# Chunk bounds of k from rows of half chunks and k's score operand by DMA, for half of the head pairs of a fused attention and feed-forward kernel

## The chip, the cores and the metric

The kernel runs on one core of one Trainium2 chip. The metric is the time on the device in microseconds (us), the median of several runs. A run can also be profiled: the profile then shows one execution, with every instruction of the five engines (PE, the matrix engine; DVE, the vector engine; ACT, the scalar engine; POOL, the general engine; SP, which here only issues transfers) and every transfer.

## The reference

The program is a chunk-selecting attention, whose output feeds a gated feed-forward layer. Batch B = 4, heads H = 8, sequence S = 768, head width D = 64, feed-forward width 1536.

```python
k_min, k_max = k_chunks.min(axis=3), k_chunks.max(axis=3)     # chunks of 32 rows of k
ub = sum_d(max(q * k_min, q * k_max))                         # per query and chunk, then a causal mask
top_chunks = argsort(ub)[..., -6:]                            # the 6 best chunks of each query
scores = (q @ k.T) / 8, kept where the chunk is chosen and the position is causal
attn = softmax(scores) @ v
x = attn with the heads side by side: 3072 tokens of 512
xn = x / sqrt(mean(x*x) + 1e-6) * rms_g
out = (silu(xn @ w_gate) * (xn @ w_val)) @ w_out
```

## The kernel before

The work is cut into 16 pairs of heads (four pairs a batch) and 8 halves of a batch for the feed-forward layer (`f0.0`, `f0.1`, ... `f3.1`). Every step (`Step`) names the engine or engines that may do it, a guess of its duration, what it depends on and the buffers that it opens and uses. A planner (`Order.run`) walks through a modelled time and, whenever an engine is free, gives it the ready step of the lowest rank; a rank is a place from `TIMES` plus an offset per kind from `RANK`. The result is one fixed instruction order per engine, which the chip then follows in order. `SLOTS` says how many buffers of each kind there are, and a step cannot be planned while its buffer is taken.

`prep` readies a pair, here for both k and q:

- `kload`, `qload`: two transfers on SP's queue bring the two heads' rows, 128 positions on the partitions, into a `nat` buffer (line 479).
- `kT`, `qT`: six fp32 transposes on PE (line 498) into PSUM, and `kE`, `qE`: two evictions by ACT or DVE (lines 294 and 298), so that d lies on the partitions: 64 rows for each of the two heads, 768 columns (`kt`, `qt`).
- `kmx`, `kmn`: two reductions on DVE over the chunks of `kt` (lines 524 and 526), then `dif`.
- `kC`, `qC`: four casts on POOL (line 298) into the bf16 operands of the scores, `KE` and `QS`. The 64 other rows of `KE` hold a constant 0 / -30000 pattern `e_all`, those of `QS` the selection.
- `relu`, `ub`, `ubE`, `up`, `ubm`, `max`, `sel`, `selT`, `selC`: the bounds, the six best chunks of each query, and the selection turned into `QS`.

`scores` then does the score matmuls (`sc`, line 718), the exponential on ACT (`exp`, line 735), and attention times v (`av`, line 754); `norm_out` divides (`xb`). `norm` scales the rows of half a batch (`sq`, `eps`, `root`, `xs`) and turns them, for batch 0 by PE (`tp`, line 848), for the others by DMA transposes on SP's queue (`xT`, line 837). `ffn` does the feed-forward matmuls (`gate` line 882, `val` line 903, `po` line 923), with `tanh` on ACT and `tg`, `hh` on DVE.

PE also has 48 steps `busy` (line 341): matmuls of zeros of 512 columns with a rank of 1000 and more, which the planner puts wherever nothing else is ready for PE; all of them fall in the first 29 us. The first feed-forward matmul waits for the first half of batch 0, that is for the scores of the first four pairs, so the kernel has a first stage without the large matmuls.

Of the kernel before, what the change touches and what calls it, by code (L numbers as in the profile page):

```python
# [8 lines left out]
FP32 = mybir.dt.float32  # L9
BF16 = mybir.dt.bfloat16  # L10
ALU = mybir.AluOpType
ACT = mybir.ActivationFunctionType
AXX = mybir.AxisListType.X
# [11 lines left out]

RANK = (
    dict(
        av=156.13, dif=-333.01, eps=-30.9, exp=-297.75, kC=249.04, kE=-171.16, kT=-97.43,
        kload=1.5, kmn=-85.09, kmx=75.56, max=-238.74, qC=324.63, qE=-109.16, qT=-140.07,
        qload=45.82, relu=246.29, root=261.37, sc=129.21, sel=17.88, selC=51.2, selT=55.02,  # L30
        sq=-363.37, tp=-68.78, tpE=108.05, ub=-155.85, ubE=-484.91, ubm=-159.09, up=-350.79,
        vload=-102.18, xb=-100.78, xs=-3.48,
    ),
    dict(
        av=8.1, dif=164.62, eps=-549.11, exp=227.88, gate=-37.01, hh=-145.73, kC=-36.47,
        kE=243.85, kT=-61.3, kload=39.2, kmn=324.05, kmx=284.92, mask=143.91, max=194.96,
        out=-122.32, po=137.5, poE=216.04, qC=234.68, qE=-450.99, qT=88.22, qload=32.32,
        relu=163.99, root=-883.1, sc=-22.64, sel=-113.94, selC=20.01, selT=-328.58, sq=384.43,
        tanh=51.44, tg=-50.58, ub=10.99, ubE=298.61, ubm=-119.37, up=-28.2, val=-0.94,
        vload=151.14, xT=-62.62, xb=39.12, xs=-64.22,  # L40
    ),
)

TIMES = {
# [15 lines left out]
}  # L60


# [139 lines left out]
def kernel(  # L202
# [11 lines left out]
    nc = tc.nc  # L214
    P = nc.NUM_PARTITIONS
    B, H, S, D = q.shape
    assert (P, D) == (128, 64) and S == 768
    CH = 32
    NCH = S // CH
    NT = S // P  # L220
# [6 lines left out]
    KM = D + NCH + 1  # L227
    W = S // 2
    G = 3
    NPAIRS = B * NP  # L230

    SLOTS = dict(ps=8, nat=8, vext=4, set=3, ku=3, selq=3, qt=7, ubs=2, small=8, ubm=3,
                 pt=10, xb=2, xt=2, row=3, xs=4, ff=8, hh=36, ob=3)

    def limits(sub, t):
        return LIMITS[sub][0 if t < FIRST else 1]
# [4 lines left out]
    WHOLE, HALVES = [(0, NT)], [(0, HB), (HB, HB)]  # L241
    PARTS = [WHOLE] * 3 + [HALVES] + [WHOLE] * (NPAIRS - NP)
    FIRST = 42.0
    BUSY = 48
    LIMITS = dict(score=(5, 3), av=(2, 2), prep=(4, 3), ffn=(3, 4), norm=(3, 2), po=(2, 2))
    order = Order(SLOTS, limits)
    order.LIM = LIMITS
# [3 lines left out]
    def add(name, engs, occ, rank, *a, **kw):  # L251
        return order.add(name, engs, occ, rank if isinstance(rank, dict) else {"": rank}, *a, **kw)

    def rank(place, b, kind, n=0, pace=None):
        r = {place: 1.0, f"{kind}.{min(b, 1)}": 1.0}
        if n:
            r[pace] = float(n)
        return r
# [14 lines left out]
    def tile_of(b, shape, dtype, name):  # L273
        pool = ps if b.kind == "ps" else sb
        b.tile = pool.tile(shape, dtype, name=name, tag=f"{b.kind}{b.slot}")
        return b.tile
# [11 lines left out]
    def pe(n):  # L288
        return 0.003 + n / 2400.0
# [20 lines left out]


    KU = [const.tile([P, 2, CH], FP32, name=f"ku{i}") for i in range(SLOTS["ku"])]
    SELQ = [const.tile([P, NT, 2, D], BF16, name=f"selq{i}") for i in range(SLOTS["selq"])]
    VX = [const.tile([P, 2 * NT, D + 1], BF16, name=f"vx{i}") for i in range(SLOTS["vext"])]
    e_all = const.tile([D, S], BF16, name="e_all")
# [19 lines left out]
    zeros = const.tile([P, 4 * P], BF16, name="zeros")  # L335
    c_zero = add("zeros", "DVE", 0.2, -101, lambda e: nc.vector.memset(zeros[:], 0.0))

    def busy(bank):
        def go(e):
            t = tile_of(bank, [P, 4 * P], FP32, "busy")  # L340
            nc.tensor.matmul(t[:], zeros[:, 0:P], zeros[:], start=True, stop=True)  # L341
        return go

    for i in range(BUSY):
        bank = Buf("ps")
        add("busy", "PE", pe(4 * P), 1000.0 + i, busy(bank), [c_zero], opens=[bank])
    c_ku = [add("ku0", "DVE", 0.1, -95 + i, lambda e, i=i: nc.vector.memset(KU[i][:], 0.0))
            for i in range(SLOTS["ku"])]
    c_sel = [add("selq0", "DVE", 0.38, -90 + i, lambda e, i=i: nc.vector.memset(SELQ[i][:], 0.0))
# [27 lines left out]
    c_e = prev  # L377
    c_ke = [None] * NB
    for i in range(NB):
        if i == 0:  # L380
            c_ke[i] = add("ke0", "", {"DVE": 1.05, "ACT": 1.4}, {"ke0": 1.0}, lambda e: (
                evict(e, KE[0][0][D:2 * D, :], e_all[:]),
                evict(e, KE[0][1][0:D, :], e_all[:])), [c_e])
        else:
            c_ke[i] = add("ke", "SP", 1.0, {"ke": 1.0}, lambda e, i=i: (
                nc.sync.dma_start(out=KE[i][0][D:2 * D, :], in_=e_all[:]),
                nc.sync.dma_start(out=KE[i][1][0:D, :], in_=e_all[:])), [c_e], load=180000)

    def make_cmf(n):
        if n == 0:  # L390
# [71 lines left out]
    def prep(c, i0, nb, at, lr):  # L462
# [4 lines left out]
        c0, c1 = i0 * 4, (i0 + nb) * 4  # L467
        nat, big = {}, {}
        done = {}
        for w, src in (("k", k), ("q", q)):  # L470
            nat[w], big[w] = Buf("nat"), Buf("qt")

            def load(e, w=w, src=src, r0=0, rn=nb):
# [44 lines left out]
        def red(e, which, x0, xn):  # L518
            view = big["k"].tile[:, x0 * P:(x0 + xn) * P].rearrange("p (c t) -> p c t", t=CH)
            a0, a1 = x0 * 4, (x0 + xn) * 4  # L520
            if which == 0:
                if mx.tile is None:
                    tile_of(mx, [P, NCH], FP32, "kmx")
                nc.vector.tensor_reduce(out=mx.tile[:, a0:a1], in_=view, axis=AXX, op=ALU.max)
            else:
                nc.vector.tensor_reduce(out=KU[c.ku.slot][:, 0, c0 + a0:c0 + a1], in_=view,
                                        axis=AXX, op=ALU.min)

        reds = []
        step = 3 if p == 0 else nb  # L530
        for x0 in range(0, nb, step):
            after = done["k"][x0 // 3:(x0 + step) // 3]
            lead = {"": -10.0} if p == 0 and x0 == 0 else {}
            reds += [
                add("kmx", "DVE", 0.06 + step * P * 0.00106, {**rank(at, b, "kmx"), **lead},
                    lambda e, x0=x0: red(e, 0, x0, step), after, opens=[mx], uses=[big["k"]]),
                add("kmn", "DVE", 0.06 + step * P * 0.00106, {**rank(at, b, "kmn"), **lead},
                    lambda e, x0=x0: red(e, 1, x0, step), after + c_ku, opens=[c.ku],
                    uses=[big["k"]])]

        def diff(e):
            engine[e].tensor_tensor(
# [5 lines left out]
        c.dif[i0] = df  # L548


        casts = []
        for w, dst in (("k", KE), ("q", QS)):
            for hl in range(2):
                rows = slice(hl * D, (hl + 1) * D)

                def cast(e, w=w, dst=dst, hl=hl, rows=rows):
                    evict(e, dst[c.set.slot][hl][rows, cols], big[w].tile[rows, 0:n])

                casts.append(add(w + "C", "", {e: {"POOL": pool(n), "ACT": act(n)}[e] for e in CASTS[p]},
                                 rank(at, b, w + "C", hl, "step"), cast, done[w], opens=[c.set],  # L560
                                 uses=[big[w]]))
# [131 lines left out]
    def scores(c, i0, nb, at, pace, adds):  # L693
# [3 lines left out]
        for hl in range(2):  # L697
# [5 lines left out]
            for g, (nd, regions) in enumerate(groups):  # L703
# [9 lines left out]
                def score(e, regions=regions, sc=sc, hl=hl, kk=kk, tri=tri):  # L713
# [9 lines left out]
                    if tri:  # L723
# [3 lines left out]
                            start=False, stop=True)  # L727

                need = list(c.sel) + [y for z in c.ke.values() for y in z] + [c_tri] + c_ke
                s = add("sc", "PE", sum(pe(x[2] * P) for x in regions) + (pe(tri * P) if tri else 0),  # L730
                        rank(at, b, "sc", m, pace), score, need, opens=[sc], uses=[c.set])

                def soft(e, sc=sc, pt=pt, nn=nn):
# [14 lines left out]
                def prod(e, pt=pt, todo=todo, av=av, left=left, hl=hl):  # L748
# [4 lines left out]
                    for m, (x, kb, qi) in enumerate(todo):  # L753
# [4 lines left out]

                avs.append(add("av", "PE", 0.029 * nn, rank(at, b, "av", m, pace), prod, [x, c.vload], opens=[av],
                               uses=[pt, c.v]))  # L760

            def norm_out(e, hl=hl, av=av):
                if XB[b].tile is None:
# [222 lines left out]
```

## Time and profile before

| what | value |
|---|---|
| median of 3 runs | 325.68 us (325.23 to 325.82) |
| time of the profiled execution | 326.77 us |
| its span, first to last instruction | 325.1 us |
| mean granted clock of PE | 0.989 |
| PE busy | 316.8 us (97%) |
| DVE busy | 245.1 us (75%) |
| ACT busy | 201.5 us (62%) |
| POOL busy | 118.8 us (37%) |
| HBM read, written | 28.57 MB, 6.29 MB |

[...] The time of the profiled execution lies 1.67 us above its span and 1.09 us above the median.

### The profile page before, as it was taken

What the parts mean: (1) busy time and instruction counts of PE and PEld (TensorE: products, weight loads), DVE (VectorE), ACT (ScalarE), POOL (GpSimd) and SP (SyncE); (2) the same over time, 40 slices, a digit from 0 to 9 for tenths busy, and PEclk for the clock granted to TensorE, in tenths of its full rate; (3) what the DMA queues carried; (4) which work ended last, traced back from release to release, by engine and by line L of the source; (5) the groups of instructions that cost most, each with busy time, mean ns of one, the idle gap of its engine ahead of it and who ended that gap; (6) DMA issues with size and microseconds to landing.
All of it is one profiled execution on the core that took longest, in us unless ns stands there. A gap on an engine that the chain in (4) does not pass through costs nothing.

```text
span 325.1 us, 7875 instructions
## 1 busy us (share of the span) xinstructions
PE 316.8 (97%) x2972; PEld 200.5 (62%) x2972; DVE 245.1 (75%) x664; ACT 201.5 (62%) x434; POOL 118.8 (37%) x170
## 2 busy tenths in 40 slices
PE   8999998999999999999999999999999999999995
PEld 3567865667667767765667667556665466555542
DVE  6789988799789889879998767969767778444500
ACT  5578988575777498993469779755465252333121
POOL 8649426364425764583213556520012000000000
PEclk9999997899999999999999999999999999999999
DMA  9999999798908669857010330150000720011023
GB/s 172 213 216 198 180 198 219 118 191 143 92 0 184 87 106 169 149 140 50 1 50 2 24 28 2 40 123 35 0 2 33 131 65 1 34 65 66 1 79 114
DMA packets 92501, 30.25 MB, mean 93 GB/s; under 512 B 85424, under 2 KB 89264, under 8 KB 92464
## 3 DMA queue, kind: packets, MB, share of 16 engines
q1 hardware_dynamic: 62352, 21.50, 29.8%
q0 software_dynamic: 28512, 7.87, 24.0%
q10 hardware_dynamic: 1600, 0.39, 0.6%
q8 instruction: 23, 0.38, 0.5%
q14 instruction: 14, 0.11, 0.1%
HBM read 28.57 MB, written 6.29 MB: 107 GB/s over the span
## 4 chain that ended last, share of the span: by engine, by line
PE 92%; DVE 4%; DMA 1%; ACT 1%; issue 0%; ACTq 0%
PE gp L882 20%; PE vp L903 19%; PE po L923 19%; PE sc L718 11%; PE av L754 6%; PE ub L586 5%; PE pq L498 3%; PE pk L498 3%; PE busy L341 3%; PE up L610 2%; PE st L655 2%; DMA qnat<-in_q_dram 1%; DVE selq L644 1%; PE tp L848 0%; DVE selq L639 0%
## 5 line engine op out<-in xcount | busy, mean ns | idle before, releaser
L735 ACT ACTIVATE pt<-sc 128x512 bf16<-128x512 f32 (+3 forms) x192 | 90.9, 570 | 7.4 <-PE sc L718 5.2
L889 ACT ACTIVATE sg<-gp 128x384 bf16<-128x384 f32 x96 | 46.9, 493 | 53.1 <-PE gp L882 52.3
L882 PE MATMUL gp<-xT,wg 128*128 128x384 bf16 x384 | 76.1, 331 | 0.0
L903 PE MATMUL vp<-xT,wv 128*128 128x384 bf16 x384 | 75.7, 326 | 0.0
L895 DVE SCALAR_TENSOR_TENSOR tg<-sg,gp 128x384 bf16<-128x384 bf16 x96 | 51.7, 550 | 25.7 <-ACT sg L889 24.8
L923 PE MATMUL po<-wo,hh 128*128 128x512 bf16 x288 | 69.2, 379 | 0.0
L911 DVE TENSOR_TENSOR hh<-vp,tg 128x384 bf16<-128x384 f32 x96 | 52.3, 553 | 9.7 <-PE vp L903 8.6
L718 PE MATMUL sc<-qs,ke 89*128 89x128 bf16 (+5 forms) x420 | 56.7, 256 | 0.5 <-ACT qs L294 0.4
L882 PEld LDWEIGHTS <-wg 128*128 128x128 bf16 x384 | 36.9, 99 | 25.2 <-issue 2.4
L903 PEld LDWEIGHTS <-wv 128*128 128x128 bf16 x384 | 36.0, 98 | 23.1 <-issue 0.8
L741 POOL TENSOR_SCALAR_AFFINE_SELECT pt<-pt 128x512 bf16<-128x512 bf16 (+1 forms) x48 | 26.1, 556 | 63.3 <-ACT pt L735 62.8
L923 PEld LDWEIGHTS <-hh 128*128 128x128 bf16 x288 | 27.3, 98 | 26.7
L754 PE MATMUL av<-vx,pt 128*128 128x65 bf16 x672 | 38.9, 193 | 1.3 <-ACT pt L735 1.3
L754 PEld LDWEIGHTS <-pt 128*128 128x128 bf16 x672 | 32.4, 98 | 10.6 <-ACT pt L735 2.2
L718 PEld LDWEIGHTS <-ke 89*128 89x128 bf16 (+1 forms) x420 | 30.9, 99 | 10.2 <-issue 2.1
L298 POOL CAST qs<-qt 64x768 bf16<-64x768 f32 x30 | 28.3, 944 | 24.3 <-DVE qt L298 13.3
L298 POOL CAST ke<-kt 64x768 bf16<-64x768 f32 x31 | 26.5, 855 | 8.3 <-ACT kt L294 5.9
L296 ACT ACTIVATE osb<-po 128x512 f32<-128x512 f32 x19 | 11.3, 597 | 29.2 <-PE po L923 29.2
L294 ACT ACTIVATE qs<-st 64x768 bf16<-64x768 bf16 x20 | 16.1, 804 | 7.5 <-PE st L655 7.2
L826 DVE SCALAR_TENSOR_TENSOR xs<-xb,ri,gains 128x512 bf16<-128x512 bf16 x24 | 18.3, 797 | 1.5 <-DMA xT<-xs 1.0
L770 DVE TENSOR_TENSOR xb<-av,rden 128x384 bf16<-128x384 f32 (+1 forms) x34 | 18.2, 534 | 1.2
L631 DVE MAX8 m<-ubm 128x8 f32<-128x24 f32 x192 | 18.9, 169 | 0.1
(72 smaller groups left out, 335.8 us busy)
## 6 DMA issues: line engine op xcount, KB each, us to landing
out_dram<-osb SPq DMA_DIRECT2D x24, 256.0 KB, 2.2
knat<-in_k_dram SPq DMA_DIRECT2D x30, 192.0 KB, 4.8
qnat<-in_q_dram SPq DMA_DIRECT2D x30, 192.0 KB, 4.9
vx<-in_v_dram POOLq DMA_DIRECT2D x16, 192.0 KB, 5.2
wo<-in_moe_w_out_dram POOLq DMA_DIRECT2D x2, 768.0 KB, 9.3
wg<-in_moe_w_gate_dram POOLq DMA_DIRECT2D x2, 768.0 KB, 8.8
wv<-in_moe_w_val_dram POOLq DMA_DIRECT2D x2, 768.0 KB, 9.3
ke<-e_all SPq DMA_DIRECT2D x4, 96.0 KB, 3.4
```

The source lines that it names most:

```text
L298: engine[e].tensor_copy(out_, in_)
L498: nc.tensor.transpose(t[:, j * P:(j + 1) * P], nat[w].tile[:, j0 + j].rearrange("p h d -> p (h d)"), ident_f[:])
L718: nc.tensor.matmul(t[:, x:x + m, :].rearrange("p a b -> p (a b)"), ke[kk, kb * P:(kb + 1) * P], qs[kk, q0 * P:(q0 + m) * P], start=not tri ...
L735: nc.scalar.activation(out=t[:, 0:nn, :], in_=sc.tile[:, 0:nn, :], func=ACT.Exp, scale=SCALE)
L741: nc.gpsimd.affine_select(out=pt.tile[:, 0:nd, :], in_=pt.tile[:, 0:nd, :], compare_op=ALU.is_ge, fill=0.0, base=0, pattern=[[0, nd], [1, ...
L754: nc.tensor.matmul(av.tile[:, qi - i0, :], pt.tile[:, x, :], VX[c.v.slot][:, hl * NT + kb, :], start=(begin and m == 0), stop=(left[0] == ...
L882: nc.tensor.matmul(t[:], wg[:, g, hs], XT[b].tile[:, g, cols], start=(g == 0), stop=(g == NP - 1))
L889: nc.scalar.activation(out=t[:], in_=gp.tile[:], func=ACT.Tanh, scale=0.5)
L895: nc.vector.scalar_tensor_tensor(out=t[:], in0=sg.tile[:], scalar=1.0, in1=gp.tile[:], op0=ALU.add, op1=ALU.mult)
L903: nc.tensor.matmul(t[:], wv[:, g, hs], XT[b].tile[:, g, cols], start=(g == 0), stop=(g == NP - 1))
L911: nc.vector.tensor_tensor(out=t[:], in0=vp.tile[:], in1=tg.tile[:], op=ALU.mult)
L923: nc.tensor.matmul(po.tile[:], hhs[ht].tile[:, th * P:(th + 1) * P], wo[:, ht, :], start=(ht == 0), stop=(ht == NHT - 1))
```

## The change

For the last 8 of the 16 pairs (`p >= ROWS`, with `ROWS = 8`) the steps `kload`, `kT`, `kE`, `kmx`, `kmn` and `kC` are replaced:

- `khload` brings the two heads' k as 96 partitions of 16 whole rows each (half a chunk per partition), 1024 numbers of fp32.
- `kmx`, `kmn` reduce each partition over its 16 rows; the reduction reads every 64th number. Their 96 x 128 result is turned by one fp32 transpose on PE, and `join`, four small reductions on DVE, makes the chunks' bounds of the half chunks' and puts them where `dif` and `ub` expect them.
- `kbload` brings k a second time, by two casting transfers on POOL's queue, into the bf16 buffer `KB`, whose other columns hold the pattern `e_all` turned (`eT`, `eC`, done once).
- `kX`: two DMA transposes on SP's queue write `KE` from `KB`, all 128 rows.

After the second head's scores of the third pair come 40 more `busy` matmuls of 256 columns, again of a rank of 1000 and more. All numbers in `RANK` and `TIMES` are new, so the order of everything changes; so are some counts of buffers. The built program has 48 fp32 transposes fewer and 8 others more on PE, 16 casts fewer on POOL, 16 evictions of k fewer on ACT and DVE together.

```diff
-    SLOTS = dict(ps=8, nat=8, vext=4, ..., qt=7, ubs=2, small=8, ubm=3,
-                 pt=10, xb=2, xt=2, row=3, xs=4, ff=8, hh=36, ob=3)
+    ROWS = 8
+    HC = S // (CH // 2)
+    SLOTS = dict(ps=8, nat=6, kh=2, km=2, kb=2, vext=4, ..., qt=6, ubs=2, small=7, ubm=3,
+                 pt=10, xb=2, xt=2, row=2, xs=4, ff=8, hh=30, ob=3)
-    BUSY = 48
+    BUSY, LATER = 48, 40
...
+    KB = [const.tile([P, 2, NT, 2 * D], BF16, name=f"kb{i}") for i in range(SLOTS["kb"])]
+    def turn_e(e):
+            nc.tensor.transpose(t[:, j], e_all[:, j * P:(j + 1) * P], ident_b[0:D, 0:D])
+    def copy_e(e):
+                evict(e, KB[i][:, h, :, (1 - h) * D:(2 - h) * D], et.tile[:])
...
-        for w, src in (("k", k), ("q", q)):
+        rows_k = p >= ROWS
+        for w, src in (("q", q),) if rows_k else (("k", k), ("q", q)):
...
+            def load_h(e):
+                t = tile_of(kh, [2 * HC, CH // 2, D], FP32, "khalf")
+                nc.sync.dma_start(out=t[:], in_=k[b, h0:h0 + 2].rearrange(
+                    "h (c t) d -> (h c) t d", t=CH // 2))
+            def whole(e, which):
+                nc.vector.tensor_reduce(
+                    out=km.tile[:, which], in_=kh.tile[:].rearrange("p t d -> p d t"), axis=AXX,
+                    op=ALU.max if which == 0 else ALU.min)
+            def turn_m(e):
+                nc.tensor.transpose(t[:], km.tile[:].rearrange("p m d -> p (m d)"),
+                                    ident_f[0:2 * HC, 0:2 * HC])
+            def join(e):
+                for m in range(2):
+                    for h in range(2):
+                        nc.vector.tensor_reduce(
+                            out=dst, in_=kt.tile[m * D:(m + 1) * D, h * HC:(h + 1) * HC].rearrange(
+                                "p (c t) -> p c t", t=2),
+                            axis=AXX, op=ALU.max if m == 0 else ALU.min)
+            def load_b(e):
+                for h in range(2):
+                    nc.gpsimd.dma_start(
+                        out=KB[kb.slot][:, h, :, h * D:(h + 1) * D],
+                        in_=k[b, h0 + h].rearrange("(t p) d -> p t d", p=P))
+                def move(e, hl=hl):
+                    nc.sync.dma_start_transpose(
+                        out=KE[c.set.slot][hl][:].rearrange("d (t p) -> d t p", p=P),
+                        in_=KB[kb.slot][:, hl].rearrange("p t d -> p (t d)"))
...
+            if p == 2 and hl:
+                for i in range(LATER):
+                    bank = Buf("ps")
+                    add("busy", "PE", pe(2 * P), 1000.0 + i, busy(bank, 2 * P), [last_sc], opens=[bank])
```

More of the change, by code (lines that the diff above doesn't have):

```diff
@@ L27 @@
     dict(
[L28 to L32, printed above, removed]
+        av=43.57, dif=-30.29, eps=179.06, exp=-200.01, kC=120.21, kE=-311.62, kT=-305.1,
+        kload=-105.22, kmn=-185.9, kmx=-27.69, max=-21.8, qC=182.72, qE=166.19, qT=-206.09,
+        qload=-84.21, relu=243.91, root=91.35, sc=-70.23, sel=-65.8, selC=94.24, selT=-324.14,
+        sq=169.36, tp=-132.93, tpE=221.19, ub=-176.21, ubE=-58.41, ubm=-542.64, up=-208.33,
+        vload=-353.61, xb=196.99, xs=-231.93,
     ),
     dict(
[L35 to L40, printed above, removed]
+        av=-55.49, dif=107.31, eps=-219.18, exp=76.29, gate=-52.44, hh=-476.39, join=12.45,
+        kC=221.56, kE=-131.64, kT=36.75, kX=16.24, kbload=-12.11, khload=45.16, kload=89.93,
+        kmn=249.43, kmx=151.07, mask=-188.09, max=127.02, out=-169.48, po=80.53, poE=187.61,
+        qC=167.85, qE=-80.09, qT=54.86, qload=78.72, relu=-304.43, root=-329.97, sc=64.55,
+        sel=15.85, selC=-282.78, selT=-64.95, sq=-40.96, tanh=168.5, tg=-70.57, ub=-23.31,
+        ubE=-254.01, ubm=22.75, up=-154.86, val=-25.56, vload=159.79, xT=-132.02, xb=55.59,
+        xs=92.8,
     ),
@@ L229 @@
     G = 3
+    ROWS = 8
+    HC = S // (CH // 2)
     NPAIRS = B * NP
-    SLOTS = dict(ps=8, nat=8, vext=4, set=3, ku=3, selq=3, qt=7, ubs=2, small=8, ubm=3,
-                 pt=10, xb=2, xt=2, row=3, xs=4, ff=8, hh=36, ob=3)
+    SLOTS = dict(ps=8, nat=6, kh=2, km=2, kb=2, vext=4, set=3, ku=3, selq=3, qt=6, ubs=2, small=7, ubm=3,
+                 pt=10, xb=2, xt=2, row=2, xs=4, ff=8, hh=30, ob=3)
     def limits(sub, t):
@@ L336, with busy @@
     c_zero = add("zeros", "DVE", 0.2, -101, lambda e: nc.vector.memset(zeros[:], 0.0))
-    def busy(bank):
+    def busy(bank, n):
         def go(e):
             t = tile_of(bank, [P, 4 * P], FP32, "busy")
-            nc.tensor.matmul(t[:], zeros[:, 0:P], zeros[:], start=True, stop=True)
+            nc.tensor.matmul(t[:, 0:n], zeros[:, 0:P], zeros[:, 0:n], start=True, stop=True)
         return go
@@ L345 @@
         bank = Buf("ps")
-        add("busy", "PE", pe(4 * P), 1000.0 + i, busy(bank), [c_zero], opens=[bank])
+        add("busy", "PE", pe(4 * P), 1000.0 + i, busy(bank, 4 * P), [c_zero], opens=[bank])
     c_ku = [add("ku0", "DVE", 0.1, -95 + i, lambda e, i=i: nc.vector.memset(KU[i][:], 0.0))
@@ L387 @@
                 nc.sync.dma_start(out=KE[i][1][0:D, :], in_=e_all[:])), [c_e], load=180000)
+    et = Buf("ps", "prep")
+    def turn_e(e):
+        t = tile_of(et, [P, NT, D], BF16, "et")
+        for j in range(NT):
+            nc.tensor.transpose(t[:, j], e_all[:, j * P:(j + 1) * P], ident_b[0:D, 0:D])
+    def copy_e(e):
+        for i in range(SLOTS["kb"]):
+            for h in range(2):
+                evict(e, KB[i][:, h, :, (1 - h) * D:(2 - h) * D], et.tile[:])
+    c_et = add("eT", "PE", 0.2, {"eT": 1.0}, turn_e, [c_e, c_idb], opens=[et])
+    c_kb = [add("eC", "", {"DVE": 4 * 0.28, "ACT": 4 * 0.39}, {"eT": 1.0}, copy_e, [c_et], uses=[et])]
     def make_cmf(n):
@@ L527, in red @@
                                         axis=AXX, op=ALU.min)
[L529 to L539, printed above, removed]
+        reds, casts = [], []
@@ L548, in prep @@
         c.dif[i0] = df
-        casts = []
-        for w, dst in (("k", KE), ("q", QS)):
+        for w, dst in (("q", QS),) if rows_k else (("k", KE), ("q", QS)):
             for hl in range(2):
@@ L729, in scores @@
                 need = list(c.sel) + [y for z in c.ke.values() for y in z] + [c_tri] + c_ke
-                s = add("sc", "PE", sum(pe(x[2] * P) for x in regions) + (pe(tri * P) if tri else 0),
+                s = last_sc = add("sc", "PE", sum(pe(x[2] * P) for x in regions) + (pe(tri * P) if tri else 0),
                         rank(at, b, "sc", m, pace), score, need, opens=[sc], uses=[c.set])
```

36 lines of the change are left out of this document (added), and 30 rows, old and new, of the table TIMES.

## The prediction

> **What bounds the kernel now.** I read the busy shares, the 40 slices and the end of the chain first, then busy time by stretches.
>
> ```profile
> PE 316.8 (97%) x2972; PEld 200.5 (62%) x2972; DVE 245.1 (75%) x664; ACT 201.5 (62%) x434; POOL 118.8 (37%) x170
> PEclk9999997899999999999999999999999999999999
> PE 92%; DVE 4%; DMA 1%; ACT 1%; issue 0%; ACTq 0%
> ```
>
> PE is busy all the time and carries 92% of the chain; the granted clock dips in slices 7 and 8. The stretches (us; busy PE, PEld, DVE, ACT, POOL; then granted clock, DMA share, GB/s) say where PE is not full:
>
> ```profile
> 40.00:48.00 8.00, 7.59 (x128) 5.78 (x127) 7.17 (x29) 6.93 (x16) 1.77 (x3) 1.00 1.08 199
> 48.00:52.00 4.00, 2.47 (x32) 1.45 (x29) 3.73 (x11) 2.99 (x9) 2.94 (x3) 1.00 1.16 201
> 52.00:54.00 2.00, 1.63 (x11) 1.10 (x10) 1.47 (x2) 1.98 (x4) 1.01 (x2) 0.56 1.15 206
> 54.00:58.00 4.00, 4.00 (x23) 2.58 (x22) 2.49 (x8) 3.85 (x10) 1.64 (x3) 0.50 1.25 239
> 58.00:60.00 2.00, 2.00 (x11) 1.05 (x10) 1.11 (x2) 1.01 (x4) 0.24 (x1) 0.73 1.15 201
> 60.00:210.00 150.00, 150.00 (x1645) 101.34 (x1644) 131.11 (x370) 110.76 (x247) 75.89 (x104) 1.00 0.54 79
> ```
>
> Before 60 us, DVE and ACT are almost full and PE waits: 1.5 us of 48 to 52. Then the clock falls to one half, until about 59. From 60 us on PE has no gap: there the time is the sum of PE's matmuls. DVE is next, 131.1 of 150 us (87%), with 18.9 us left; that number decides below. The timeline shows what opens the second stage:
>
> ```profile
> 50.84 2.63 DVE L826 SCALAR_TENSOR_TENSOR xs<-xb,ri,gains 128x512 bf16<-128x512 bf16 x3
> 51.64 0.40 PE L848 MATMUL tp<-ident_b,xs 128*128 128x128 bf16 x4
> 54.92 0.63 PE L848 MATMUL tp<-ident_b,xs 128*128 128x128 bf16 x4
> 55.59 0.42 DVE L298 COPY xT<-tp 128x512 bf16<-128x512 bf16 x1
> 56.06 5.20 PE L882 MATMUL gp<-xT,wg 128*128 128x384 bf16 x22
> ```
>
> The three `xs` end at 53.47; the later transposes stand on PE behind scores at half clock, and the first `gate` starts at 56.06. So the time is the start of `gate`, then PE's remaining work, then a tail after the last matmul that the change does not touch (an eviction and a store).
>
> **The change part by part.** The prices on PE:
>
> ```profile
> 74.82 0.82 PE L498 MATMUL pk<-ident_f,knat 128*128 128x128 f32 x6
> 63.37 0.49 PE L498 MATMUL pk<-ident_f,knat 128*128 128x128 f32 x3
> L724 PE MATMUL sc<-trimask,ident_b 128*128 128x512 bf16 x6 | 2.3, 380 | 0.0
> L724 PE MATMUL sc<-trimask,ident_b 128*128 128x256 bf16 x6 | 1.6, 274 | 0.0
> ```
>
> Three more fp32 transposes take 0.33 us: 0.11 each. 256 more bf16 columns take 106 ns: 0.053 us per 128.
>
> *PE after the first gate.* The program's order says what stands behind the first `gate`. Before, the k transposes of pairs 5 to 15, 66 of them; after, those of pairs 6 and 7, 12, and 8 single ones: 54 x 0.11 = 5.9 us less, 8 x 0.11 = 0.9 more. The first eight score groups of pair 4 (29 blocks of 128 columns) stood ahead of the gate and now stand behind: 29 x 0.053 = 1.5 more. So does the `selT` of pair 4, six blocks: 0.3 more. The half clock after 56.06 (to about 59) cost 1.5 us, which goes if the clock stays full. Sum: -5.9 + 0.9 + 1.5 + 0.3 - 1.5 = -4.7 us.
>
> *The 40 zero matmuls.* 40 x 0.106 = 4.2 us of PE. In the order nine lie among the scores of pair 3 and 31 between its last `av` and the first `tp`, that is in the wait for `xs`. PE's other work ahead of the first `tp` changes by +0.2 (`eT`) and -0.3 (`selT`). Before, PE got to the first `tp` at 51.6 (the row above), having waited 1.5 us in that stretch; 51.6 - 1.5 + 4.2 - 0.1 = 54.2, where the first `xs` would be ready at 50.84 + 0.88 = 51.7 and the third at 53.5. So the zeros cover the wait and cost at most 0.7 us past the third `xs`; without the wait they would cost all 4.2.
>
> *The start of gate.* DVE does more ahead of `xs`: four copies for `eC`, priced by the copy to `xT` below at 0.42 each, 1.7 us; the other steps moved over this line (four evictions of q fewer, four of bounds more, two sums of squares more, two `max` and a `sel` fewer) come to about nothing. With all 1.7 the third `xs` ends at 55.2, and `tp` and a copy at full clock, 0.8, put the gate at 56.0. With none of it, and the zeros, 55.0. Before it was 56.06. I take no change.
>
> *DVE behind it.*
>
> ```profile
> L524 DVE TENSOR_REDUCE kmx<-kt 128x24 f32<-128x768 f32 x15 | 14.1, 943 | 0.7 <-ACT kt L294 0.4
> L524 DVE TENSOR_REDUCE kmx<-kt 128x12 f32<-128x384 f32 x2 | 1.1, 543 | 0.0
> L298 DVE COPY kt<-pk 128x384 f32<-128x384 f32 x8 | 4.4, 555 | 4.4 <-PE pk L498 3.9 <-PE av L754 0.3
> L298 DVE COPY xT<-tp 128x512 bf16<-128x512 bf16 x2 | 0.8, 424 | 1.3 <-PE tp L848 1.3
> L644 DVE TENSOR_SCALAR selq<-m x16: 181/190/858, 16.9 to 221.7; 128x12 bf16<-128x12 f32 x16
> L810 DVE TENSOR_SCALAR ms<-ss x8: 157/169/170, 48.7 to 249.6; 128x3 f32<-128x3 f32 x8
> ```
>
> Between 384 and 768 numbers a reduction grows by 400 ns: 1.04 ns a number over 143 ns. Sixteen reductions of 1024 numbers take 16 x 1.21 = 19.4 us in place of 16 x 0.943 = 15.1. But they read every 64th number. No row has a long strided read. The nearest are the last two: 12 numbers at a stride take a median of 190 ns, 3 adjacent ones 169; 21 ns for nine more, 2.3 ns each, and here the write is strided too. So a reduction lies between 1.21 us and 143 + 1024 x 2.09 = 2.28 us, the double slope; nothing excludes a little more, and less than the contiguous price is excluded because the count of numbers sets it. I take the lower end for the forecast, since twelve numbers are a thin row, and keep the upper one as a rival. `join` is four tiny operations of about 0.17 us (the 169 ns row): 8 x 0.7 = 5.6. Five evictions move from DVE to ACT or go, -2.8. Sum +7: 138 of 150 us, 92%; PE stays the bound. ACT loses 15 evictions of k and gains nine others, so it is no bound.
>
> *POOL and SP.*
>
> ```profile
> L298 POOL CAST ke<-kt 64x768 bf16<-64x768 f32 x31 | 26.5, 855 | 8.3 <-ACT kt L294 5.9 <-DVE kt L298 1.2 <-PE sc L718 0.2
> L456 POOL DMA_DIRECT2D vx<-in_v_dram x16 | 16.8, 1050 | 5.3 <-PE up L610 2.6 <-PE av L754 2.2 <-issue 0.4
> L837 SPq DMA_TRANSPOSE xT<-xs x18: 1190/1216/1682, 130.7 to 260.2; - x18
> DMA to landing us min/median/max: 2.4/2.4/4.0
> ```
>
> POOL drops 16 casts (13.7 us) and issues 16 casting loads of half of `vx`'s size, 0.5 to 1.05 us each, 8 to 17 us: no bound at 76 of 150. A DMA transpose of four blocks occupies SP's queue 1.2 us and lands after 2.4; six blocks by proportion 1.8 and 3.6. A pair's two hold SP 3.6 us, and what waits behind them are loads of later pairs and stores of `out`. The tightest places are pairs 10 and 15, whose operand buffers the previous pair gives back about 7 us of PE work ahead of their first score: 1.8 + 3.6 = 5.4 fits. The second load of k adds about 3 MB to a stage whose DMA share is 0.54.
>
> *Sum.* 326.77 - 4.7 = 322.1 us for a profiled execution, span 320.4. The median stood 1.09 below the profiled time: **321.0 us**.
>
> **The rivals.**
>
> *Strided reductions make DVE the bound.* At 2.28 us the sixteen cost 16 x 1.07 = 17.1 us more: 131.1 + 7 + 17.1 = 155 of DVE work for 150 us of PE work. It decides from about 1.8 us a reduction on, where the 18.9 us of room are used up. PE then waits at `selT`, `po` and the feed-forward's banks: 5 us at least, 8 with two waits' worth of DVE idling left; I put 6.5, that is 327.5 us, slower. For it: the 190 ns row, and a strided memset on POOL below. Against it: both are tiny operations.
>
> ```profile
> L351 POOL MEMSET vx<- 128x12 bf16 x4 | 0.6, 144 | 0.0
> L403 POOL MEMSET trimask<- 128x128 bf16 x1 | 0.2, 197 | 0.0
> ```
>
> (12 scattered numbers take nearly as long as 128 adjacent ones.) [...]
>
> *The clock falls all the same.* PE may still idle between the three `tp` while DVE finishes `xs`, about 0.9 us apart. Before, a stretch with 2.47 of 4 us busy was enough to halve the clock, one with 7.59 of 8 was not. If it falls again, the 1.5 us are not won and up to 1.5 are lost ahead of the gate: 323 us. [...]
>
> *The transposes come late.* If six blocks land at the worst row's rate, 4.0 x 1.5 = 6 us, the two tight places and the loads queued behind cost 1 to 2 us: 322.5. That the change does not do what it says is excluded for the order (the zeros stand where they should); for the clock it is the rival above.
>
> **How the numbers follow.** Forecast 0.42, strided rival 0.38, clock 0.10, late transposes 0.05, something else 0.05. A measurement here can tell 0.2%, 0.65 us. Faster by more: 0.39 + 0.09 + 0.03 + 0.03 (a price halfway) = 0.54; the same: 0.08; slower: 0.31 of the strided rival and the unnamed 0.05 and a little = 0.38. The forecast's own range is 319.0 to 323.5 (gate 1 us earlier, zeros or small waits 2.5 us dearer); the strided rival reaches from 323.5 to 331. Together 319.0 to 329.5.
>
> **What would show it.** Right: `pk` x48, the third slice group at full clock with `gate` near 56 us, reductions near 1.2 us, DVE near 92% in 60 to 210, PE without gaps. Wrong: reductions near 2.3 us with PE waiting for DVE between 100 and 200 us; a clock below 0.9 after 50 us; scores of pairs 10 or 15 waiting for a transpose.

## The result, and the profile after

The changed kernel takes 329.91 us (median of 6 runs, 329.51 to 330.78); the kernel before took 325.9 us beside it (6 runs, 325.23 to 326.93). The ratio is 1.0117, 95% interval 1.0102 to 1.0131: slower by 1.2%. The forecast was 321.0 us, faster. The profiled execution took 330.35 us, its span is 328.6 us.

The busy shares, the granted clock, and the chain that ended last, first by engine, then by line:

```profile
PE 315.7 (96%) x2955; PEld 198.7 (60%) x2978; DVE 258.0 (79%) x690; ACT 198.4 (60%) x424; POOL 119.4 (36%) x174
PEclk9999999999999999999999999999999999999999
PE 68%; DVE 26%; issue 3%; ACT 1%; ACTq 0%
PE po L1011 15%; PE vp L991 14%; PE gp L970 13%; PE sc L801 8%; DVE kmm L564 7%; PE busy L345 5%; PE av L837 4%; DVE tg L983 4%; DVE hh L999 3%; PE ub L669 3%; PE pq L518 2%; DVE m L714 2%; DVE rt L651 2%; DVE xb L858 2%; PE pk L518 1%
```

The clock does not fall in this execution, but DVE now carries 26% of the chain where it had 4%, and the largest line of DVE in it is `kmm`, the strided reductions. Next the groups that the change adds (the number behind the bar is the busy sum, then the mean of one in ns):

```profile
L564 DVE TENSOR_REDUCE kmm<-khalf 96x64 f32<-96x1024 f32 x16 | 30.6, 1917 | 0.0
L587 DVE TENSOR_REDUCE ku<-kmt 64x24 f32<-64x48 f32 x16 | 3.4, 210 | 0.3
L587 DVE TENSOR_REDUCE kmx<-kmt 64x24 f32<-64x48 f32 x16 | 3.1, 195 | 0.1
L575 PE MATMUL kmt<-ident_f,kmm 96*128 96x96 f32 x8 | 1.9, 254 | 1.5 <-DVE rden L857 0.8 <-DVE kmm L564 0.7
```

A strided reduction takes 1.92 us where the forecast put 1.21. The stretches (us; busy PE, PEld, DVE, ACT, POOL; clock, DMA share, GB/s):

```profile
48.00:52.00 4.00, 4.00 (x62) 3.16 (x61) 3.62 (x13) 3.12 (x9) 2.34 (x3) 1.00 1.19 254
60.00:210.00 150.00, 144.40 (x1516) 93.08 (x1527) 139.94 (x380) 99.94 (x217) 71.44 (x100) 1.00 0.87 117
```

The zeros fill the wait at 48 to 52 us. Between 60 and 210 us PE, which had no gap before, lacks 5.6 us, and DVE rose from 131.1 to 139.94. Who it waits for, by the waits of PE behind the first `gate` (us in total, times, longest):

```profile
PE up L693 <- DVE ubs L301: 0.9, 2, 0.7
PE kmt L575 <- DVE rden L857: 0.8, 1, 0.8
PE sc L801 <- DVE hh L999: 0.7, 1, 0.7
PE kmt L575 <- DVE kmm L564: 0.7, 1, 0.7
PE sc L801 <- DVE qs L301: 0.6, 1, 0.6
```

Each of these is short, and most name another DVE operation than `kmm`. The same stretch on both engines shows why:

```profile
200.07 1.89 DVE L564 TENSOR_REDUCE kmm<-khalf 96x64 f32<-96x1024 f32 x1
201.89 0.17 DVE L857 RECIPROCAL rden<-av 128x6 f32<-128x6 f32 x1
202.10 0.27 PE L575 MATMUL kmt<-ident_f,kmm 96*128 96x96 f32 x1 [0.79 <-DVE rden L857]
```

The reduction ends at 201.96 and PE's transpose of its result waits for it; the wait is put down to the reciprocal that came just behind. DVE takes its steps in the planned order: the reciprocal behind this reduction (1.89 us from 200.07) starts only at 201.89, so whatever stands behind a long reduction is late with it.

The time can be split at the first `gate`:

```profile
53.23 0.39 PE L936 MATMUL tp<-ident_b,xs 128*128 128x128 bf16 x4
55.67 2.11 PE L970 MATMUL gp<-xT,wg 128*128 128x384 bf16 x12 [0.95 <-ACT xT L297]
```

`gate` starts at 55.67 (before: 56.06). From there to the end of the span it was 325.1 - 56.06 = 269.0 us; now it is 328.6 - 55.67 = 272.9. All of the loss lies behind the gate.

### The profile page after: what moved, and what is told of

It is laid out like the page before. It is cut to its first block, busy times and chain, and to the rows that moved or that the text cites. A ratio compares the mean times of both kernels' runs of the same rounds, so it can differ in the third digit from the quotient of the medians.

```text
span 328.6 us, 7911 instructions
## 1 busy us (share of the span) xinstructions
PE 315.7 (96%) x2955; PEld 198.7 (60%) x2978; DVE 258.0 (79%) x690; ACT 198.4 (60%) x424; POOL 119.4 (36%) x174
## 4 chain that ended last, share of the span: by engine, by line
PE 68%; DVE 26%; issue 3%; ACT 1%; ACTq 0%
PE po L1011 15%; PE vp L991 14%; PE gp L970 13%; PE sc L801 8%; DVE kmm L564 7%; PE busy L345 5%; PE av L837 4%; DVE tg L983 4%; DVE hh L999 3%; PE ub L669 3%; PE pq L518 2%; DVE m L714 2%; DVE rt L651 2%; DVE xb L858 2%; PE pk L518 1%
## 5 line engine op out<-in xcount | busy, mean ns | idle before, releaser
L818 ACT ACTIVATE pt<-sc 128x512 bf16<-128x512 f32 (+3 forms) x192 | 88.2, 572 | 10.1 <-PE sc L801 7.0
L1011 PE MATMUL po<-wo,hh 128*128 128x512 bf16 x267 | 66.3, 379 | 1.3 <-issue 0.3
L801 PE MATMUL sc<-qs,ke 89*128 89x128 bf16 (+5 forms) x418 | 52.4, 250 | 1.5 <-DVE hh L999 0.7
L801 PEld LDWEIGHTS <-ke 128*128 128x128 bf16 (+1 forms) x420 | 29.9, 97 | 12.8 <-issue 3.2
L837 PEld LDWEIGHTS <-pt 128*128 128x128 bf16 x672 | 30.2, 98 | 8.8 <-issue 1.2
L837 PE MATMUL av<-vx,pt 128*128 128x65 bf16 x672 | 34.4, 193 | 0.1
L301 POOL CAST qs<-qt 64x768 bf16<-64x768 f32 x30 | 27.6, 919 | 11.4 <-ACT qt L297 6.1
L564 DVE TENSOR_REDUCE kmm<-khalf 96x64 f32<-96x1024 f32 x16 | 30.6, 1917 | 0.0
L299 ACT ACTIVATE osb<-po 128x512 f32<-128x512 f32 x23 | 13.7, 603 | 27.3 <-PE po L1011 27.1
L345 PE MATMUL busy<-zeros 128*128 128x512 bf16 (+1 forms) x88 | 19.9, 355 | 1.3 <-DVE zeros L340 1.3
L301 POOL CAST ke<-kt 64x768 bf16<-64x768 f32 x15 | 12.8, 851 | 17.6 <-DVE kt L301 13.2
```

Source lines behind the costliest of these rows:

```text
L301: engine[e].tensor_copy(out_, in_)
L345: nc.tensor.matmul(t[:, 0:n], zeros[:, 0:P], zeros[:, 0:n], start=True, stop=True)
L564: nc.vector.tensor_reduce(out=km.tile[:, which], in_=kh.tile[:].rearrange("p t d -> p d t"), axis=AXX, op=ALU.max if which == 0 else ALU.min)
L801: nc.tensor.matmul(t[:, x:x + m, :].rearrange("p a b -> p (a b)"), ke[kk, kb * P:(kb + 1) * P], qs[kk, q0 * P:(q0 + m) * P], start=not tri ...
L818: nc.scalar.activation(out=t[:, 0:nn, :], in_=sc.tile[:, 0:nn, :], func=ACT.Exp, scale=SCALE)
L837: nc.tensor.matmul(av.tile[:, qi - i0, :], pt.tile[:, x, :], VX[c.v.slot][:, hl * NT + kb, :], start=(begin and m == 0), stop=(left[0] == ...
```

## The experiments

The first theory was the prediction's own rival: the strided reductions make DVE late, and PE waits. Against it stood the clock and the zeros, the second load of k with its transposes, and the new order by itself.

**Contiguous reductions.** Each reduction reads 16 adjacent numbers in place of 16 rows, so the bounds are of other numbers; nothing else changes, the order included.

```diff
-                    out=km.tile[:, which], in_=kh.tile[:].rearrange("p t d -> p d t"), axis=AXX,
+                    out=km.tile[:, which], in_=kh.tile[:].rearrange("p t d -> p (t d)").rearrange(
+                        "p (d t) -> p d t", t=CH // 2), axis=AXX,
```

> The changed kernel with one edit: the sixteen reductions of the half chunks read 16 adjacent numbers in place of every 64th, same count of numbers, same program order (the bounds are those of other numbers, so the selection is not the reference's). Theory 1 (the price of the strided read: 1.92 us measured against 1.21 by the contiguous slope, 16 x 0.71 = 11 us of vector-engine work in a stage without room): a reduction takes 1.2 us, PE's waits between 60 and 210 us nearly go, 321 to 323 us. Theory 2 (the new order with its longer chains, or the second load of k, makes PE wait whatever a reduction costs): the reductions get shorter and the time stays 328 to 330 us.

322.72 us (322.63 to 323.75), ratio 0.9913, interval 0.9889 to 0.9937, as theory 1 expected. The engines' shares of its chain, its reductions, its stretch, its first `gate`, and the longest of PE's waits behind it:

```profile
PE 92%; DVE 2%; ACT 2%; DMA 1%; issue 1%; POOL 1%; ACTq 0%
L564 DVE TENSOR_REDUCE kmm<-khalf 96x64 f32<-96x1024 f32 x16 | 19.2, 1206 | 0.0
60.00:210.00 150.00, 148.22 (x1592) 98.26 (x1604) 135.29 (x404) 105.72 (x229) 76.26 (x104) 1.00 0.89 117
55.02 0.65 PE L971 MATMUL gp<-xT,wg 128*128 128x384 bf16 x3 [0.95 <-ACT xT L297]
PE av L838 <- POOL pt L825: 0.4, 1, 0.4
```

16 x (1.917 - 1.206) = 11.4 us of DVE make 329.91 - 322.72 = 7.2 us of time. With the contiguous price the kernel would be faster than before by 0.9%. Both kernels have the same order on PE, so their matmuls can be matched one by one. Behind the first `gate` the changed kernel falls 7.0 us behind (272.9 against 265.9), 5.5 us of it at eight places where PE stands and a DVE result releases it, 0.3 to 0.95 us each. This one address pattern is what turns the sign.

**No later zeros.** The 40 zero matmuls of 256 columns are left out, the order is kept.

```diff
+            if n < 4 * P:
+                return
```

> The changed kernel without its 40 later zero matmuls, all else in the same order. Theory 1 for the clock (the zeros fill a wait and keep the clock full): the granted clock falls to one half somewhere between 50 and 60 us and the time rises by 2 to 3.5 us, to 332 to 333.5 us. Theory 2 (the clock would have stayed up in this order anyway, and the zeros are dead weight or free): no dip, 329 to 330 us.

330.67 us (329.89 to 331.74), ratio 1.0152, interval 1.0119 to 1.0185. The four runs fall in two groups: 329.89 and 329.95 at a mean clock of 0.999, 331.39 and 331.74 at 0.988 and 0.989. The profiled one, of the first group, kept its clock though PE was half idle:

```profile
48.00:52.00 4.00, 1.94 (x36) 1.00 (x24) 3.92 (x14) 2.90 (x8) 2.13 (x3) 1.00 1.19 257
```

So the zeros themselves cost nothing that shows (329.9 with them), and without them two of four executions have a lower clock and take 1.6 us more, somewhat less than theory 1 put. They are not the loss.

**Zeros in the kernel before.** 26 zero matmuls of 256 columns are put by hand into PE's waits around the last `av` of pair 3.

```diff
+    put = dict(zip(avs, (8, 3, 3, 3)))
+    put[next(i for i in at if named(i, "selT", "a4"))] = 2
+    put[next(i for i in at if named(i, "tp", "n0.0"))] = 2
+    put[next(i for i in at if named(i, "sc", "s4.0"))] = 5
```

> The kernel before with 26 zero matmuls of 256 columns (2.8 us of PE) put into its planned order where PE waited between 48 and 52.5 us: 8, 3, 3, 3 ahead of the last four av of pair 3, 2 ahead of selT of pair 4, 2 ahead of the first tp, 5 ahead of the first sc of pair 4. No other step moves. Theory 1 (the half clock after 52 us cost 3.3 us of PE work and comes from those waits): clock stays at 1.0, 322.5 to 323.5 us. Theory 2 (the stage is set by DVE and ACT, and the clock there costs little): clock up, time 325 to 326 us. If the zeros themselves come late: 326 to 327.

327.54 us (326.77 to 327.92), ratio 1.0049, interval 1.003 to 1.0068: a little slower, at a mean clock of 0.997 to 1.0, and above all three expected ranges. The stretches that ran at a clock of 0.56 and 0.50 before:

```profile
52.00:54.00 2.00, 1.94 (x26) 1.55 (x24) 1.34 (x2) 1.02 (x2) 0.88 (x2) 1.00 1.16 210
54.00:58.00 4.00, 3.63 (x34) 2.50 (x35) 2.41 (x7) 4.00 (x9) 1.01 (x2) 1.00 1.20 231
```

The clock is kept and no time is won: here the zeros cost more than they bring. They come late, as the third range supposed: the first `tp` starts at 52.98 in place of 51.64 and the first `gate` at 56.57 in place of 56.06, and behind it PE waits 0.9 us where it had no wait.

**Elementwise trees in place of the strided reductions.** Maximum and minimum are made by operations on adjacent rows, which read contiguously; in the second kernel the nine operations of both trees alternate, at the place of `kmn`.

```diff
-                nc.vector.tensor_reduce(
+                    nc.vector.tensor_tensor(out=y[:, 0:8], in0=y[:, 0:8], in1=y[:, 8:16], op=op)
+                    nc.vector.tensor_tensor(out=y[:, 0:4], in0=y[:, 0:4], in1=y[:, 4:8], op=op)
+                nc.vector.tensor_tensor(out=y[:, 0:2], in0=y[:, 0:2], in1=y[:, 2:4], op=op)
+                nc.vector.tensor_tensor(out=km.tile[:, which], in0=y[:, 0], in1=y[:, 1], op=op)
```

> The changed kernel with each of the sixteen strided reductions replaced by a tree of elementwise max or min over adjacent numbers (960 numbers in four or five operations, about 1.3 us by the contiguous slope, against 1.92), same result as the reference, same order otherwise. Theory 1 (price of the strided read): 16 x 0.6 = 10 us of vector-engine work less, 322 to 324 us, faster than before. Theory 2 (order and chains): 328 to 330 us.

> The changed kernel with the two strided reductions of a pair replaced by two trees of elementwise max and min over adjacent numbers whose nine operations alternate, so that none waits for the one just ahead of it; all stand where the second reduction stood; result as the reference. By the contiguous slope 1.3 us a tree, 2.6 a pair against 3.84. Theory 1: 10 us less on the vector engine than the changed kernel, 323.5 to 325 us, faster than before. [...]

331.63 us (331.22 to 331.9), ratio 1.0178, interval 1.0157 to 1.0199, and 333.0 us (332.15 to 333.73), ratio 1.0185, interval 1.0162 to 1.0208. Both lie above every range that was expected. The four operations of a minimum's tree in the first of them, over the eight pairs:

```profile
L574 DVE TENSOR_TENSOR khalf<-khalf 96x512 f32<-96x512 f32 x8 | 5.4, 677 | 0.0
L575 DVE TENSOR_TENSOR khalf<-khalf 96x256 f32<-96x256 f32 x8 | 3.7, 460 | 0.3
L576 DVE TENSOR_TENSOR khalf<-khalf 96x128 f32<-96x128 f32 x8 | 2.7, 339 | 0.3
L577 DVE TENSOR_TENSOR kmm<-khalf 96x64 f32<-96x64 f32 x8 | 2.1, 256 | 0.3
```

Together 1.73 us; the five operations of a maximum's tree take 2.15, so a pair pays 3.89 us against 2 x 1.92 = 3.83. From 64 to 512 numbers an operation grows by 421 ns, 0.94 ns a number, which leaves about 0.2 us of each operation that does not depend on the count. By this estimate the fixed parts of nine operations eat the gain of the contiguous reading. In the second kernel the nine operations take 3.57 us a pair, less than the two reductions, and yet the time is 2 to 3 us longer (by the ratios, by the medians); why is open.

**A list of prices.** The pairs 8 to 14 read their 1024 numbers at strides of 1, 2, 4, 8, 16, 32 and 64 numbers, pair 15 two adjacent numbers at each 64th; the bounds are then of other groups of numbers.

```diff
+                st = {8: 1, 9: 2, 10: 4, 11: 8, 12: 16, 13: 32, 14: 64}[p]
+                view = kh.tile[:].rearrange("p t d -> p (t d)").rearrange(
+                    "p (o t s) -> p o s t", o=D // st, s=st)
```

> A price list, read from the durations alone: in the changed kernel the two reductions of pairs 8 to 14 read 1024 numbers at a stride of 1, 2, 4, 8, 16, 32 and 64 numbers of 4 bytes (pair 8: 1, pair 9: 2, pair 10: 4, 11: 8, 12: 16, 13: 32, 14: 64), and those of pair 15 read two adjacent numbers at each 64th (the bounds of these pairs are those of other numbers). [...] Theory 2 (the long stride of 256 bytes is what costs, a conflict): 1.21 up to stride 16 or 32, 1.92 at 64. Theory 3: any stride costs, 1.92 from 2 on.

Times in the timeline, in the order of strides 1, 2, 4, 8, 16, 32, 64 and the two adjacent ones (start us, duration us):

```profile
137.71 1.21 DVE L575 TENSOR_REDUCE kmm<-khalf 96x64 f32<-96x1024 f32 x1
93.25 1.21 DVE L575 TENSOR_REDUCE kmm<-khalf 96x64 f32<-96x1024 f32 x1
159.73 2.03 DVE L575 TENSOR_REDUCE kmm<-khalf 96x64 f32<-96x1024 f32 x1
133.56 2.03 DVE L575 TENSOR_REDUCE kmm<-khalf 96x64 f32<-96x1024 f32 x1
116.46 1.88 DVE L575 TENSOR_REDUCE kmm<-khalf 96x64 f32<-96x1024 f32 x1
106.47 1.93 DVE L575 TENSOR_REDUCE kmm<-khalf 96x64 f32<-96x1024 f32 x1
171.70 1.91 DVE L575 TENSOR_REDUCE kmm<-khalf 96x64 f32<-96x1024 f32 x1
180.12 1.21 DVE L566 TENSOR_REDUCE kmm<-khalf 96x32 f32<-96x1024 f32 x1
```

The price is a step, not a slope: 1.21 us up to a stride of 8 bytes, 1.88 to 2.03 from 16 bytes on, with no growth to 256 bytes. Neither theory 2, with the step at the longest strides, nor theory 3, with the step at 2 numbers, holds. With two neighbours read at each place the stride of 256 bytes costs nothing more, 1.21 us. Over the 143 ns of the contiguous rows that is 1.04 and about 1.73 ns a number; the whole reduction takes 1.6 to 1.7 times as long. Why the step lies between 8 and 16 bytes, no run shows. The kernel ran once, 325.6 us, which says nothing of its time.

**Strided reductions in the kernel before.** For the last eight pairs its own reductions read at a stride of 24 numbers, so that each chunk holds other positions.

```diff
+                "p (c t) -> p c t", t=CH) if p < 8 else big["k"].tile[:].rearrange(
+                "p (t c) -> p c t", t=CH)
```

> The kernel before, where the reductions of the last 8 pairs read their 768 numbers at a stride of 24 numbers instead of adjacent ones (other bounds, so another selection); nothing else changes. By the measured slope 143 + 768 x 1.73 ns = 1.47 us in place of 0.94: 16 x 0.53 = 8.4 us more on the vector engine, 139.5 of 150 us between 60 and 210. Theory 1 (what counts is the room left on the vector engine there, 18.9 us): most is hidden, 327 to 330 us. Rival (each reduction lies on the path of its pair): the whole 8 us show, 333 to 335 us.

337.85 us (337.07 to 341.44), ratio 1.0321, interval 1.0304 to 1.0338, above both expected ranges. The profiled execution is the slowest, 341.44 us at a clock of 0.974.

```profile
L526 DVE TENSOR_REDUCE kmx<-kt 128x24 f32<-128x768 f32 x15 | 23.0, 1531 | 0.5 <-ACT kt L294 0.4
```

Seven of the 15 are contiguous at 0.943 us, so the eight others took (15 x 1.531 - 7 x 0.943) / 8 = 2.05 us: 16 x 1.1 = 17.7 us more of DVE, where 8.4 were expected, make 11 us more of time. By theory 1, 131.1 + 17.7 = 148.8 of 150 us, they would have been hidden; the rival, in which each reduction lies on the path of its pair, is nearer. The mechanism shows without any other part of the change. The price, (2.05 - 0.14) / 768 = 2.5 ns a number, is above the 1.73 of the list; why is open.

**The second load of k once only.** The casting load is issued for the first two of the eight pairs; the later ones score with those pairs' k.

```diff
-                for h in range(2):
+                once.append(kb.slot)
+                for h in range(2 if once.count(kb.slot) == 1 else 0):
```

> The changed kernel in which the casting load of k is issued only for the first two of the eight pairs; the six others transpose what lies in the buffer (so their scores are those of other keys). Leaves 12 of 16 transfers of 96 KB out, and their issue on POOL. Theory 1 (vector engine): 329 to 330.5 us as the changed kernel. Rival (the second load of k crowds the transfers, DMA share 0.87 against 0.54, or POOL's issues delay the masks): 2 us or more faster, 326 to 328.

329.63 us (329.31 to 329.98), ratio 1.0083, interval 1.0068 to 1.0098, and 0.3 us under the changed kernel. The kernel before took 326.8 us beside it, where it took 325.9 beside the changed kernel, so by the ratios the difference is at most 1.1 us. The load, its traffic and its issue on POOL are not the loss.

**The planner with the true price.** Only the planner's cost of a strided reduction is altered, 1.90 us in place of 1.15.

```diff
-            w_x = add("kmx", "DVE", 0.06 + o * D * 0.00106, rank(at, b, "kmx"),
+            w_x = add("kmx", "DVE", 0.06 + o * D * 0.0018, rank(at, b, "kmx"),
```

> The changed kernel with one thing altered: the planner's own cost of a strided reduction of 1024 numbers is 1.90 us, as measured, in place of 1.15. The instructions are the same in kind; the plan gives some more of the shared work to ACT (on DVE two evictions of q, two of the selection, three of the bounds and three sums of squares fewer, some 5 us of DVE). Theory 1 (the loss of about 7 us is DVE's work standing ahead of PE, partly because the order was made with a price of 60%): PE's idle time behind the first gate falls from 6.1 to 2 to 4 us and the time is 326 to 328.5 us. Rival (DVE is simply full and an order cannot help, or ACT's extra work is late in its turn): 329 to 331 us.

335.94 us (334.71 to 337.18), ratio 1.0289, interval 1.0262 to 1.0317. Both expectations fail: it is 6 us slower than with the wrong price.

```profile
170.00:185.00 15.00, 11.01 (x160) 6.64 (x159) 13.96 (x43) 13.47 (x31) 9.42 (x15) 1.00 0.54 83
185.00:200.00 15.00, 12.01 (x152) 8.73 (x153) 12.48 (x52) 7.33 (x17) 4.65 (x9) 0.77 0.43 61
PE ub L669 <- DVE ku L587: 2.5, 2, 1.9
PE kmt L575 <- DVE kmm L564: 2.1, 2, 1.1
```

In this order PE stands still for 7 of 30 us near the last pairs, waiting for their bounds, and the clock falls as well, to a mean of 0.77 in the second of these stretches. The ranks stayed those that came with the lower cost. Which of the moved steps does it was not tried.

**The new form for fewer pairs.** `ROWS` is 10 or 12, with the planner's cost at 1.90 and 1.80 us.

```diff
-    ROWS = 8
+    ROWS = 12
```

> The changed kernel with the new form of k for the last 6 pairs (ROWS = 10) in place of 8, and the planner's cost of a strided reduction at 1.90 us. Each pair that goes back to the old form costs PE 5 transposes more, 0.55 us, and spares DVE two times 0.97 us of strided reading and 0.8 us of joins, less up to 0.55 us of eviction: 2.2 to 2.7 us. Theory 1 (the time is PE's work plus the stalls that a full DVE makes): PE +1.1 us, DVE -5 us, stalls of about 2 us: 324 to 327 us, near the kernel before. Rival (stalls come from the places of single reductions and not from their sum): the six pairs left still stall PE by 4 to 6 us, 328 to 330 us.

> The changed kernel with the new form of k for the last 4 pairs (ROWS = 12) in place of 8, and the planner's cost of a strided reduction at 1.80 us. Theory 1: against the contiguous variant, 322.7 us, where PE bounds, PE gets 4 x 0.55 = 2.2 us more; DVE has 4 x 2.2 to 2.7 = 9 to 11 us less than in the changed kernel and is back near 87 to 90% of the second stage, so stalls are about 1 us: 324 to 326 us, about the kernel before or up to 0.5% under it. Rival (stalls come from the places of single reductions): 327 to 329 us.

`ROWS = 10`: 335.8 us (334.94 to 336.13), ratio 1.0281, interval 1.0255 to 1.0307, above both expected ranges. Its stretch, and the longest wait of PE, behind 210 us, a feed-forward half whose operand is late:

```profile
60.00:210.00 150.00, 148.24 (x1571) 97.90 (x1585) 137.71 (x386) 107.10 (x228) 70.96 (x98) 1.00 0.84 110
PE gp L970 <- DMA xT<-xs: 5.6, 1, 5.6
```

With twelve reductions PE lacks 1.8 us of the 150, as much as in the contiguous variant. What it loses against the changed kernel is mostly this one wait, an order which leaves PE without work at one place, so the time tells little of the number of pairs. `ROWS = 12`: 326.9 us (12 runs, 326.16 to 327.17), ratio 1.002, interval 1.0006 to 1.0034.

```profile
60.00:210.00 150.00, 147.51 (x1579) 97.70 (x1590) 136.79 (x384) 108.70 (x237) 72.86 (x101) 1.00 0.73 100
```

With eight strided reductions in place of sixteen most of the loss is gone, and so is most of the gain on PE: about the kernel before, 0.9 us above the range of theory 1 and just under that of the rival. Of all kernels that ran several times only the contiguous variant, whose bounds are of other numbers, is faster than the kernel before.

**The kernel before, once more.** Nothing is altered but a comment.

> The kernel before once more, unchanged, for a second profile. Theory (the half clock of the first profile is chance and hides behind waits that were there anyway): a granted clock near 1.0 with no fall behind 50 us, the first gate at 55 to 56 us and 264 to 266 us of PE behind it, time 325 to 326.5 us. Rival (the half clock cost the 1.5 us that the prediction gave it): with a full clock the span is 1.5 us shorter, 323.6 us, and the time 324.5 to 325.3 us.

326.41 us, at a clock of 0.988: the clock fell again, about a microsecond earlier in the same wait.

```profile
48.00:52.00 4.00, 2.70 (x34) 1.81 (x32) 3.73 (x11) 2.83 (x8) 2.66 (x3) 0.86 1.16 202
```

So this run can't compare the two profiles, but the 33 runs of the kernel before beside the experiments can. Sixteen have a mean clock of 0.988 to 0.990 and take 326.83 us on the mean (326.4 to 327.33), 17 have 0.993 or more and take 325.76 (324.99 to 326.41). So the low clock goes with 1.1 us more, and about half of the executions have it (2 of 9, 6 of 7 and 8 of 17 in the three sets). Among the 17, nine at 0.993 or 0.994 take no longer than eight at 0.998 or more: 325.59 against 325.96. The profiled execution of the prediction (0.989, 326.77 us) was one of the sixteen's kind.

## Why the prediction was wrong

The step that failed is the price of the reductions in *DVE behind it*. The text bounded it by 1.21 and 2.28 us and took the lower end "since twelve numbers are a thin row". The row was thin but right in direction: a reduction took 1.92 us. The double slope of the upper end, 2.09 ns a number, was an estimate; the runs gave about 1.73 on 96 partitions and 2.5 on 128. This one term is worth 7.2 us of the 8.9 between 321.0 and 329.91.

A second step failed with it: that DVE's work costs nothing until it fills the 150 us. The text has this decide "from about 1.8 us a reduction on", but its own figures give 1.95: of the 18.9 us of room its +7 leaves 11.9, which is 0.74 for each of sixteen reductions. At 1.92 the sum would be 131.1 + 7 + 16 x 0.71 = 149.5 us, and nothing would be lost. In the run DVE stood at 139.94 of 150 us, 93%, and PE already lacked 5.6 us. Taken in five parts, the stage is not even (columns as above):

```profile
60.00:90.00 30.00, 29.57 (x256) 19.41 (x255) 26.25 (x66) 19.86 (x42) 16.07 (x21) 1.00 0.80 105
90.00:120.00 30.00, 28.33 (x363) 18.71 (x365) 28.34 (x78) 21.17 (x48) 14.29 (x21) 1.00 0.77 84
120.00:150.00 30.00, 29.79 (x253) 18.17 (x255) 27.16 (x69) 16.84 (x40) 16.83 (x22) 1.00 1.35 184
150.00:180.00 30.00, 28.31 (x283) 17.32 (x285) 28.96 (x76) 20.15 (x40) 8.92 (x13) 1.00 0.83 147
180.00:210.00 30.00, 28.40 (x367) 19.47 (x368) 29.24 (x96) 21.92 (x50) 15.33 (x24) 1.00 0.57 64
```

PE lacks 1.6 to 1.7 us in each of the three parts where DVE is busy 28.3 us or more, and little in the two others. Here room in one part did not help another, and in a fixed order each reduction of 1.92 us delays what stands behind it.

The other 1.7 us come from the base. The forecast for a profiled execution was 322.1; the contiguous variant, which has the price that the forecast assumed, gave 322.63 profiled and 322.72 in the median. Its median does not lie 1.09 below its profiled time, because the 1.09 was most likely the half clock of the one execution of before that was profiled: the runs above put it at 1.1. The sum took the half clock off as -1.5, and then again as the distance to the median: 1.1 us counted twice. The remaining 0.6 is in the terms.

Point by point:

- *PE after the first gate*, -4.7: the contiguous variant has 320.9 - 55.02 = 265.9 us behind the gate against 269.0, so -3.1, small waits included. *The start of gate*, no change: 55.02 there and 55.67 in the changed kernel against 56.06. Together -4.2 of span for -4.7 forecast. The count of 54 fewer transposes, and PE as the bound at the contiguous price, were right.
- *Zero matmuls*, at most 0.7 us: right, 329.9 with and without them where the clock holds. They do keep the clock: 0.998 to 1.0 in all six runs of the changed kernel, against 0.988 and 0.989 in two of the four without them. But what they save is 1.1 to 1.6 us in about half of the executions, not 1.5 in each.
- *`join`*, 0.7 us a pair: 4 x 0.2 = 0.8.
- *POOL and SP*, no bound: right. A casting load lands after 4.4 us in the median, a DMA transpose after 4.0 where 3.6 was estimated, and no score waits for one.

```profile
kb<-in_k_dram POOLq DMA_DIRECT2D x16, 96.0 KB, 4.4
ke<-kb SPq DMA_TRANSPOSE x16, 4.0
```

- *The strided rival*: its mechanism is what happened, also in size (6.5 us put, 7.2 measured, though the reductions are shorter than it assumed). It supposed that the loss is DVE's work beyond 150 us, and that did not happen: the waits came without it. Its time of 327.5 was low by the 1.7 us of the base and 0.7 of these waits.
- *Clock falls again* and *transposes late*: neither came.

Shown: the price of the stride, and that it makes the loss (one pattern altered, with the same order, and PE's lost time found at waits for DVE). Shown too: that neither the zeros nor the second load do. Not settled: why other orders of nearly the same work lose 6 us more, why the second pair of trees is slower with less work on DVE, and why a stride of 96 bytes on 128 partitions costs more than 256 bytes on 96.

## What to carry to other kernels

When a change turns a reduction's address pattern, price it by a run or by its worst bound, not by the contiguous slope: here 1024 numbers took 1.21 us up to a stride of 8 bytes, 1.88 to 2.03 from 16 bytes on, and 1.21 again with two neighbours read at each place. Room on an engine, summed over a stage, is no cover for longer operations in a fixed order: here 10 us of it were left on DVE and PE still waited. Where an unknown price decides between two signs, a thin row that points one way is evidence, and the absence of a thick one is none. Before a stall or a slow clock in one profiled execution is taken off, see whether the other runs have it at all; otherwise it is counted once in the sum and once in the step to the median.

## What the runs showed of the hardware

- A reduction of 1024 fp32 numbers on each of 96 partitions took 1.21 us on DVE at strides of 4 and 8 bytes, 1.88 to 2.03 us at the five strides from 16 to 256 bytes, and 1.21 us with two adjacent numbers read at each 256 bytes. On 128 partitions a stride of 96 bytes cost 2.05 us for 768 numbers, against 0.94 for adjacent ones.
- An elementwise operation on two fp32 inputs took 0.26 us for 64 numbers a partition and 0.68 for 512 on the mean, so a pair's two trees of four and five operations, 3.89 us, bring nothing against two strided reductions, 3.83.
- In 16 of 33 executions of one and the same program the mean granted clock was 0.988 to 0.990, and they took 1.1 us more; in the two that were profiled it fell to one half in the same wait. PE was busy 2.47 of the 4 us ahead of the first of these falls; a stretch of the changed kernel without its later zeros, with PE busy 1.94 of 4 us, kept the full clock in one execution. What sets off a fall, and why about half of the executions have it, no run shows.
